# Reordering VectorE's work in a two-layer MLP behind chunked attention, with another loading of the first heads and earlier first matmuls

## The chip, the cores and the metric

The kernel runs on one core of a Trainium2 chip. The metric is the device time of one execution in microseconds (us), as the median over several runs. The engines are called PE (TensorE: matmuls and transposes), ACT (ScalarE), DVE (VectorE), POOL (GpSimd) and SP (SyncE, which here only starts DMAs). Each works through its own list of instructions in order; they wait for each other through semaphores. SBUF is the on-chip memory that all read and write, PSUM the small memory into which PE writes.

## The reference

Attention over chunks, for 4 batches, 8 heads, 768 positions and 64 elements per head; each chunk of 32 queries sees 16 positions to the left, its own 32, 8 to the right and 8 memory rows. Then an MLP over the 3072 tokens with 512 inputs and 2048 hidden units.

```
for c in range(nc):                       # 24 chunks of 32
    l_start, r_end = max(0, 32*c - 16), min(S, 32*c + 32 + 8)
    k_full = concatenate([mem_k, k[:, :, l_start:r_end]], axis=2)
    v_full = concatenate([mem_v, v[:, :, l_start:r_end]], axis=2)
    a = softmax(q_c @ k_full.T / sqrt(64))
    out[:, :, 32*c:32*c + 32] = a @ v_full
x = out.transpose(0, 2, 1, 3).reshape(3072, 512)
h = x @ w_in                              # 512 -> 2048
s = sin(alpha * h)
g = h + s * s / (alpha + 1e-09)
return g @ w_out                          # 2048 -> 512, fp32
```

## The kernel before

The work goes batch by batch, 768 tokens each. Three kinds of stage follow one another.

**Attention burst** (`burst`). Eight blocks of 96 queries (three chunks each). Per block, `qk_exp` makes scores on PE (tile `sc`) and exponentials on ACT (`pt`); `pv` multiplies with v on PE (`ot`) and normalizes on DVE (`rinv`, `x_blk`); `xt` transposes the result on PE and DVE copies it into `xT`, the MLP's input, 96 columns at a time. The three steps of one block lie `lag` iterations apart. In the burst of batch 0, a dummy matmul (`spin`, tile `z`) goes into each iteration.

**First layer** (`l1`, 16 steps, one for each 128 hidden units, called ft). Eight matmuls (4 slices of the 512 inputs, kt, times 2 halves of the tokens) fill a PSUM tile `hT`; ACT computes u = sin(alpha h); the square s2 of u is made by ACT, DVE or POOL, by a letter of a string ("A", "D", "P"; line 460); DVE combines it with `hT` to `gT` (L367). In batch 0 steps 3, 7 and 11 use two small PSUM tiles `hs` instead of `hT` (`split`).

**Second layer** (`l2`). Six blocks of 128 tokens, 16 matmuls each, into a PSUM tile `o`; each block is copied to `o_sb`, in turn by DVE (L400) and ACT (L402), and stored by SP. It is a generator: `Stream.take(n)` issues its next n matmuls, so that the second layer of a batch is spread over the next batch's transposes, burst and first layer.

What sets the order is the program's text: the schedule is written by hand, and the instructions of an engine run as they are emitted. In step ft of the first layer the order is: `stream.take` (2 matmuls of the second layer, 3 in the last batch; a finished block's copy comes with them), in batches 1 and 2 on even ft a `piece` (transposes of one head pair of k or q for the batch after: `t_k` L242 with copies to `kTi` on DVE, L243 and L249; `t_q` L257 with a copy on ACT, L258; the pairs are brought together by `pair_up`, L226, on POOL), and then the whole of `l1` with its square and `gT`.

PSUM tiles come from two pools: `big`, three buffers, holds `hT`, `sc`, `ot` and some transposes; `smp`, two buffers, holds `o`, `hs`, `z` and, in the first-layer stages, the transposes (`tt_a`). A tile that is asked for waits until the last readers of the tile that had the buffer are done: `hT` of a step waits for `gT` of three `hT` tiles before. The SBUF pool `mlp` has three buffers for each of `u`, `s2` and `o_sb`.

Almost all loads are issued by POOL[...]: k and q of batch 0 by head pairs (four of each), v of batch 0 in 16 issues (L125, L129), w_in in 8 pieces of 256 columns (L212), k and q of batch 1, w_out in 4 pieces of 4 ft each (L218), v of batch 1 in four issues (L139 to L148). These queue loads share eight semaphores in turn, and an issue waits until the load eight before it has landed. After the loads, POOL makes copies of head pairs and the "P" squares. The first pairs are brought together (`pr`) by DVE and ACT, transposed, and the burst of batch 0 begins.

Of the kernel before, what the change touches and what calls it, by code (L numbers as in the profile page):

```python
# [9 lines left out]
P = 128  # L10
# [4 lines left out]
F32 = mybir.dt.float32  # L15
ACTF = mybir.ActivationFunctionType
ALU = mybir.AluOpType
# [28 lines left out]
def kernel(  # L46
# [12 lines left out]
    nc = tc.nc  # L59
    B, H, S, D = q.shape  # L60
# [6 lines left out]
    KT = d_model // P  # L67
    NSUB = S // P
    HALF = S // 2
# [121 lines left out]
    for c0, c1, thr, val in (  # L191
# [4 lines left out]
            out=biasm[:, c0:c1], in_=biasm[:, c0:c1],  # L196
# [11 lines left out]
    for pt in pts:  # L208
        nc.vector.memset(pt[:, H * QW:H * QW + 32], 0.0)

    def load_w_in(c):
        nc.gpsimd.dma_start(  # L212
            w_in_sb[:, :, 256 * c:256 * c + 256],
            moe_w_in[:, 256 * c:256 * c + 256].rearrange("(kt p) f -> p kt f", p=P),
        )

    def load_w_out(c):
        nc.gpsimd.dma_start(  # L218
            w_out_sb[:, 4 * c:4 * c + 4, :],
            moe_w_out[512 * c:512 * c + 512].rearrange("(ft p) o -> p ft o", p=P),  # L220
        )


    def pair_up(src, hp, eng=None):
        pr = blk.tile([P, 6, 2, D], BF, name="pr")
        (eng or nc.gpsimd.tensor_copy)(  # L226
            pr[:].rearrange("p r e d -> p e r d"), src[:, 2 * hp:2 * hp + 2]
        )
        return pr

# [80 lines left out]
    def burst(b, stream, shares, lag):  # L311

        xT = xp.tile([P, KT, S], BF, name="xT")
        ptl, xbl = {}, {}
        for s in range(NJ + lag + 1):
            n = shares[s] if s < len(shares) else 0
            if s < NJ:
                ptl[s] = qk_exp(s)
            if b == 0:
                spin(1)  # L320
            stream.take(n // 3, True)
            if 0 <= s - lag < NJ:
                xbl[s - lag] = pv(b, s - lag, ptl.pop(s - lag))
# [9 lines left out]
    def l1(i, ft, xT, gT, sq, split=False):  # L333
        if split:
            hts = [smp.tile([P, 512], F32, name="hs", tag="sm") for _ in range(2)]
        else:
            hT = big.tile([P, 2, 512], F32, name="hT", tag="big")
            hts = [hT[:, 0], hT[:, 1]]
        for kt in range(KT):
            for hf in range(2):  # L340
                nc.tensor.matmul(  # L341
                    hts[hf][:, 0:HALF],
                    w_in_sb[:, kt, P * ft:P * ft + P],
                    xT[:, kt, HALF * hf:HALF * hf + HALF],
                    start=(kt == 0), stop=(kt == KT - 1),
                )
        u = mlp.tile([P, 2, HALF], F32, name="u")
        if split:
            for hf in range(2):
                nc.scalar.activation(  # L350
                    u[:, hf], hts[hf][:, 0:HALF], ACTF.Sin, scale=alpha_sb[:, ft:ft + 1])
        else:
            nc.scalar.activation(u[:], hT[:, :, 0:HALF], ACTF.Sin, scale=alpha_sb[:, ft:ft + 1])  # L353
        s2 = mlp.tile([P, 2, HALF], F32, name="s2")
        if sq == "A":
            nc.scalar.activation(s2[:], u[:], ACTF.Square)  # L356
        else:
            (nc.vector if sq == "D" else nc.gpsimd).tensor_tensor(  # L358
                out=s2[:], in0=u[:], in1=u[:], op=ALU.mult)
        gv = gT[:, ft, :].rearrange("p (e c) -> p e c", e=2)  # L360
        for hf in range(2):
            if split:
                nc.vector.scalar_tensor_tensor(
                    out=gv[:, hf], in0=s2[:, hf], scalar=inv_alpha[:, ft:ft + 1],
                    in1=hts[hf][:, 0:HALF], op0=ALU.mult, op1=ALU.add)
            elif hf == 0:
                nc.vector.scalar_tensor_tensor(  # L367
                    out=gv, in0=s2[:], scalar=inv_alpha[:, ft:ft + 1],
                    in1=hT[:, :, 0:HALF], op0=ALU.mult, op1=ALU.add)

    def l2(i, gT, last=False):
        for s in range(NSUB):
# [32 lines left out]


    first = [nc.vector.tensor_copy, nc.scalar.copy] * 2 + [nc.vector.tensor_copy] * 4
    prs = [pair_up(kq[n], 0, first[n]) for n in range(2)]
    for n in range(2 * HP):
        (t_k if n % 2 == 0 else t_q)(prs[n], n // 2)  # L410
        spin(2)
# [24 lines left out]
    xT = burst(0, stream, (), 2)  # L436
    put_memk(1)
    put_memv(1)

    for i in range(B):  # L440
        gT = gp.tile([P, FT, S], BF, name="gT")
        last = i == B - 1
        at_ft = {2 * n: n for n in range(8)}
        pieces = []
        if not last:
            srcs = [(kq_next[n % 2], n // 2) for n in range(2 * HP)]
        state["pools"] = 1

        def pair_to(n):
            while len(pieces) < min(n, 2 * HP):  # L450
                pieces.append(pair_up(*srcs[len(pieces)], nc.vector.tensor_copy if i == 0 and len(pieces) % 2 == 0 else None))

        def piece(n):
            pair_to(n + 3)
            (t_k if n % 2 == 0 else t_q)(pieces[n], n // 2)

        if 0 < i < B - 1:
            pair_to(2)
        for ft in range(FT):
            sq = ("ADADADAAADADADAA" if i == 0 else "ADAAPDADADAPADAD")[ft]  # L460
            if 1 <= ft:
                stream.take(3 if last else 2)
            if 0 < i < B - 1 and ft in at_ft:
                piece(at_ft[ft])
            if i == 0 and ft == 14:
                pair_to(3)
            l1(i, ft, xT, gT, sq, i == 0 and ft in (3, 7, 11))
        stream.add(l2(i, gT, last))
        if not last:
            if i == 0:  # L470
                state["pools"], state["t"] = 3, 0
                stream.take(4)
# [12 lines left out]
            if i + 2 < B:  # L485
                load_v_all(i + 2)
                put_memv(i + 2)
# [31 lines left out]
```

The softmax here doesn't subtract the row's maximum and nothing guards it: scores larger than these inputs give would overflow.

## Time and profile before

| | |
|---|---|
| median of 8 runs | 243.73 us (243.23 to 245.54) |
| the profiled execution, own time | 243.65 us |
| its span (first to last instruction) | 241.9 us |
| granted clock of PE | full in all slices |
| head: loads, transposes of batch 0 | 0 to 16 us |
| burst of batch 0 | 16 to 28 |
| first layer of batch 0 | 28 to 52 |
| transposes for batch 1, with second layer of batch 0 | 52 to 62 |
| burst of batch 1 / first layer | 62 to 81 / 81 to 113 |
| burst of batch 2 / first layer | 113 to 135 / 135 to 167 |
| burst of batch 3 / first layer | 167 to 189 / 189 to 217 |
| second layer of batch 3, end | 217 to 242 |

The stages are read from the timeline, from the first matmul of one kind to the first of the next. A matmul is called by its line (L341 first layer, L393 second layer, L266 scores, L288 attention times v). The page gives a mean of 326 ns for a first-layer matmul, but that is its duration from start to end in a pipeline; eight in a row take 1.30 us in the chain of waits, 0.163 us each. Of the waits, those of PE count: an idle time of another engine costs nothing unless PE waits for it later.

### The profile page before, as it was taken

To read this page: it belongs to the slowest core of one execution; us is meant where nothing else is said; L and a number is where in the kernel's file an instruction comes from. 1 tells how busy PE (TensorE), PEld (TensorE's weight loads), DVE (VectorE), ACT (ScalarE), POOL (GpSimd) and SP (SyncE) were. 2 spreads that over 40 slices of the span, in tenths; PEclk is the share of its full clock that TensorE was granted. 3 is DMA by queue.
4 is the path that set the end of the run, shared out by engine and by line. 5 is a ranking of instruction groups with operands and counts; after the bars stand their busy time and mean duration, and the time that the engine had idled before them with its cause. 6 is when DMAs were issued, how large, how long until landed. Compare 5 with 4: busy or idle time off the path is not lost.

```text
span 241.9 us, 4498 instructions
## 1 busy us (share of the span) xinstructions
PE 220.4 (91%) x1785; PEld 122.1 (50%) x1785; DVE 160.1 (66%) x287; ACT 154.5 (64%) x237; POOL 72.7 (30%) x96
## 2 busy tenths in 40 slices
PE   7698899988989979898999996998999999899994
PEld 2345465545445555454455653554455555454453
DVE  3577979998268667969557686968557267876100
ACT  3499499973884467788563774778764775871000
POOL 8899865213912114148300114120000002020000
PEclk9999999999999999999999999999999999999999
DMA  7999999999999910009994101001111101101122
GB/s 79 163 119 88 155 186 204 207 204 125 167 220 135 120 46 0 36 9 154 172 144 89 46 0 43 0 3 43 46 43 47 43 0 46 43 0 43 43 89 87
DMA packets 53852, 21.11 MB, mean 87 GB/s; under 512 B 36296, under 2 KB 50888, under 8 KB 53832
## 3 DMA queue, kind: packets, MB, share of 16 engines
q0 software_dynamic: 47616, 14.40, 73.2%
q1 hardware_dynamic: 6216, 6.43, 9.1%
q8 instruction: 14, 0.23, 0.4%
q14 instruction: 6, 0.05, 0.1%
HBM read 28.91 MB, written 6.29 MB: 146 GB/s over the span
## 4 chain that ended last, share of the span: by engine, by line
PE 44%; DMA 15%; DVE 13%; issue 11%; POOL 9%; ACT 7%; POOLq 1%; DVEq 0%; ACTq 0%
PE o L393 26%; DMA w_out_sb<-in_moe_w_out_dram 9%; PE hT L341 8%; DVE gT L367 6%; DVE s L358 4%; DMA w_in_sb<-in_moe_w_in_dram 4%; POOL vw L125 3%; ACT u L353 3%; PE ot L288 3%; PE sc L266 3%; POOL s L358 2%; DMA q_bf<-in_q_dram 2%; POOL vw L129 2%; ACT s L356 2%; ACT pt L275 2%
## 5 line engine op out<-in xcount | busy, mean ns | idle before, releaser
L393 PE MATMUL o<-w_out_sb,gT 128*128 128x512 bf16 x368 | 98.7, 380 | 1.5 <-DMA w_out_sb<-in_moe_w_out_dram 0.9
L341 PE MATMUL hT<-xT,w_in_sb 128*128 128x384 bf16 x488 | 87.5, 326 | 3.9 <-DVE gT L367 3.6
L367 DVE SCALAR_TENSOR_TENSOR gT<-s,inv_alpha,hT 128x768 bf16<-128x768 f32 x61 | 61.1, 1012 | 28.9 <-ACT s L356 20.4
L353 ACT ACTIVATE u<-hT,alpha_sb 128x768 f32<-128x768 f32 x61 | 54.6, 897 | 26.7 <-PE hT L341 25.5
L341 PEld LDWEIGHTS <-w_in_sb 128*128 128x128 bf16 x512 | 49.4, 98 | 38.7 <-issue 5.9
L275 ACT ACTIVATE pt<-sc,biasm 128x256 bf16<-128x256 f32 x96 | 37.5, 492 | 13.1 <-PE sc L266 13.1
L393 PEld LDWEIGHTS <-gT 128*128 128x128 bf16 x368 | 31.8, 98 | 26.4 <-DVE gT L367 1.4
L358 POOL TENSOR_TENSOR s<-u 128x768 f32<-128x768 f32 x6 | 8.8, 1466 | 73.7 <-ACT u L353 73.7
L356 ACT ACTIVATE s<-u 128x768 f32<-128x768 f32 x34 | 28.7, 843 | 1.1
L358 DVE TENSOR_TENSOR s<-u 128x768 f32<-128x768 f32 x24 | 24.6, 1025 | 0.4 <-ACT u L353 0.3
L293 DVE TENSOR_TENSOR x_blk<-ot,rinv 96x512 bf16<-96x512 f32 x32 | 22.0, 687 | 1.1
L226 POOL COPY pr<-q_bf 128x768 bf16<-128x768 bf16 x12 | 10.0, 837 | 41.9 <-PE tt_a L242 24.8
L292 DVE RECIPROCAL rinv<-ot 96x8 f32<-96x8 f32 x32 | 6.5, 202 | 20.0 <-PE ot L288 19.6
L402 ACT COPY o_sb<-o 128x512 f32<-128x512 f32 x11 | 6.4, 585 | 20.0 <-PE o L393 20.0
L400 DVE COPY o_sb<-o 128x512 f32<-128x512 f32 x12 | 8.3, 688 | 16.1 <-PE o L393 16.1
L288 PEld LDWEIGHTS <-pt 128*128 128x128 bf16 x256 | 11.9, 98 | 7.2 <-issue 2.3
L171 PE MATMUL z<-zeros 128*128 128x512 bf16 x37 | 13.5, 452 | 1.3 <-DVE zeros L165 1.3
L288 PE MATMUL ot<-vw,pt 128*128 128x65 bf16 x256 | 13.0, 193 | 0.8 <-ACT pt L275 0.6
L266 PEld LDWEIGHTS <-kTi 64*128 64x128 bf16 x256 | 6.9, 94 | 13.0 <-issue 6.6
L257 PEld LDWEIGHTS <-pr 128*128 128x128 bf16 x96 | 6.2, 97 | 14.1 <-issue 7.8
L266 PE MATMUL sc<-qT,kTi 64*128 64x96 bf16 x256 | 11.4, 205 | 1.8 <-ACT pt L275 1.2
L306 PEld LDWEIGHTS <-x_blk 96*128 96x128 bf16 x128 | 8.4, 97 | 6.6 <-DVE x_blk L293 1.5
(66 smaller groups left out, 181.2 us busy)
## 6 DMA issues: line engine op xcount, KB each, us to landing
out_dram<-o_sb SPq DMA_DIRECT2D x23, 256.0 KB, 2.3
k_bf<-in_k_dram POOLq DMA_DIRECT2D x3, 768.0 KB, 9.2
q_bf<-in_q_dram POOLq DMA_DIRECT2D x3, 768.0 KB, 14.0
vw<-in_v_dram POOLq DMA_DIRECT2D x6, 384.0 KB, 18.3
w_in_sb<-in_moe_w_in_dram POOLq DMA_DIRECT2D x8, 256.0 KB, 7.7
w_out_sb<-in_moe_w_out_dram POOLq DMA_DIRECT2D x4, 512.0 KB, 19.0
k_bf<-in_k_dram POOLq DMA_DIRECT2D x4, 192.0 KB, 6.0
q_bf<-in_q_dram POOLq DMA_DIRECT2D x4, 192.0 KB, 6.5
```

The costliest lines, as they stand in the source:

```text
L171: nc.tensor.matmul(z[:], zeros[:, 0:P], zeros[:])
L226: (eng or nc.gpsimd.tensor_copy)(pr[:].rearrange("p r e d -> p e r d"), src[:, 2 * hp:2 * hp + 2])
L266: nc.tensor.matmul(sc[:, e, QW * hp:QW * hp + QW], kTi[64 * e:64 * e + 64, hp, 104 * j:104 * j + P], qT[64 * e:64 * e + 64, hp, QW * j:QW ...
L275: nc.scalar.activation(pt[:, 0:H * QW].rearrange("p (g e c) -> p e g c", g=4, e=2)[:, :, :, 32 * m:32 * m + 32], sc[:, :, 0:4 * QW].rearra ...
L288: nc.tensor.matmul(otv[:, h // 4, h % 4, :], pt[:, QW * h:QW * h + P], vws[b % 2][:, h, j, 0:D + 1])
L293: nc.vector.tensor_tensor(out=x_blk[:].rearrange("p (g e) d -> p g e d", g=2), in0=otv[0:QW, :, :, 0:D], in1=rv.unsqueeze(3).to_broadcast( ...
L341: nc.tensor.matmul(hts[hf][:, 0:HALF], w_in_sb[:, kt, P * ft:P * ft + P], xT[:, kt, HALF * hf:HALF * hf + HALF], start=(kt == 0), stop=(kt ...
L353: nc.scalar.activation(u[:], hT[:, :, 0:HALF], ACTF.Sin, scale=alpha_sb[:, ft:ft + 1])
L356: nc.scalar.activation(s2[:], u[:], ACTF.Square)
L358: (nc.vector if sq == "D" else nc.gpsimd).tensor_tensor(out=s2[:], in0=u[:], in1=u[:], op=ALU.mult)
L367: nc.vector.scalar_tensor_tensor(out=gv, in0=s2[:], scalar=inv_alpha[:, ft:ft + 1], in1=hT[:, :, 0:HALF], op0=ALU.mult, op1=ALU.add)
L393: nc.tensor.matmul(o[:], gT[:, ft, P * s:P * s + P], w_out_sb[:, ft, :], start=(ft == 0), stop=(ft == FT - 1),)
```

## The change

Five things are done together.

1. `l1` no longer emits the square on DVE and `gT`. It returns them as a function `finish`, which is called in the next step after `stream.take` and `piece`, ahead of that step's matmuls (after the loop for the last step). Squares on ACT and POOL stay where they were.
2. The squares of batch 0 go from ten on ACT and six on DVE to eight on ACT, four on DVE and four on POOL. The last batch takes 2 second-layer matmuls per step instead of 3.
3. The first head pair of k and q is loaded without a cast, fp32, by SP's and ACT's queues into two buffers of the pool tag `u`; the copies to `pr` read fp32. POOL has six loads of k and q pairs left.
4. w_in is loaded in five pieces (256, 256, then three of 512 columns), w_out in two of 8 ft each.
5. In the burst of batch 0, a hook issues the first-half matmuls (4 of 8) of ft 0 and ft 1 in iteration 9 (before and after the transposes of block 6) and of ft 2 in iteration 10 (after those of block 7). `l1` later issues the other half alone.

```diff
@@ -178,7 +178,11 @@
     kq = alloc_qk()
-    load_qk_pair(0, 0, *kq)
+    kq0 = []
+    for src, eng in ((k, nc.sync), (q, nc.scalar)):
+        f = mlp.tile([P, 2, HALF], F32, name="u")
+        eng.dma_start(f[:], src[0, 0:2].rearrange("h (p r) d -> p h (r d)", p=P))
+        kq0.append(f)
     masks.make_identity(nc, ident[:])
@@ -208,23 +212,25 @@
-    def load_w_in(c):
+    def load_w_in(c0, c1):
...
-            w_out_sb[:, 4 * c:4 * c + 4, :],
-            moe_w_out[512 * c:512 * c + 512].rearrange("(ft p) o -> p ft o", p=P),
+            w_out_sb[:, 8 * c:8 * c + 8, :],
+            moe_w_out[1024 * c:1024 * c + 1024].rearrange("(ft p) o -> p ft o", p=P),
...
@@ -323,27 +329,36 @@
+            if hook:
+                hook(s, 0, xT)
             stream.take((n + 1) // 3, True)
             if 0 <= s - lag - 1 < NJ:
                 xt(xT, s - lag - 1, *xbl.pop(s - lag - 1))
+            if hook:
+                hook(s, 1, xT)
             stream.take((n + 2) // 3, True)
...
+    def l1_mm(hts, ft, xT, kt, hf):
+        nc.tensor.matmul(
+            hts[hf][:, 0:HALF],
+            w_in_sb[:, kt, P * ft:P * ft + P],
+            xT[:, kt, HALF * hf:HALF * hf + HALF],
+            start=(kt == 0), stop=(kt == KT - 1),
+        )
+
+    def l1(ft, xT, gT, sq, hts, halves, split=False):
         for kt in range(KT):
...
+            for hf in halves:
+                l1_mm(hts, ft, xT, kt, hf)
...
+        elif sq == "P":
+            nc.gpsimd.tensor_tensor(out=s2[:], in0=u[:], in1=u[:], op=ALU.mult)
+
+        def finish():
+            if sq == "D":
+                nc.vector.tensor_tensor(out=s2[:], in0=u[:], in1=u[:], op=ALU.mult)
+            gv = gT[:, ft, :].rearrange("p (e c) -> p e c", e=2)
...
+                elif hf == 0:
+                    nc.vector.scalar_tensor_tensor(
+                        out=gv, in0=s2[:], scalar=inv_alpha[:, ft:ft + 1],
+                        in1=hT[:, :, 0:HALF], op0=ALU.mult, op1=ALU.add)
+
+        return finish
...
-    for c in range(8):
-        load_w_in(c)
+    for c0, c1 in ((0, 256), (256, 512), (512, 1024), (1024, 1536), (1536, 2048)):
+        load_w_in(c0, c1)
     kq_next = load_qk(1)
-    for c in range(4):
+    for c in range(2):
         load_w_out(c)
...
+    def early(s, point, xT):
+
+        ft = {(9, 0): 0, (9, 1): 1, (10, 1): 2}.get((s, point))
+        if ft is not None:
+            opened[ft] = l1_open(ft)
+            for kt in range(KT):
+                l1_mm(opened[ft], ft, xT, kt, 0)
+
+    xT = burst(0, stream, (), 2, early)
...
+        finish = None
         for ft in range(FT):
-            sq = ("ADADADAAADADADAA" if i == 0 else "ADAAPDADADAPADAD")[ft]
+            sq = ("ADADAAPADPADPAPA" if i == 0 else "ADAAPDADADAPADAD")[ft]
             if 1 <= ft:
-                stream.take(3 if last else 2)
+                stream.take(2)
             if 0 < i < B - 1 and ft in at_ft:
                 piece(at_ft[ft])
             if i == 0 and ft == 14:
                 pair_to(3)
-            l1(i, ft, xT, gT, sq, i == 0 and ft in (3, 7, 11))
+            if finish is not None:
+                finish()
+            split = i == 0 and ft in (3, 7, 11)
+            if ft in opened:
+                finish = l1(ft, xT, gT, sq, opened.pop(ft), (1,))
+            else:
+                finish = l1(ft, xT, gT, sq, l1_open(ft, split), (0, 1), split)
+        finish()
         stream.add(l2(i, gT, last))
```

`l1_open` asks for the PSUM tiles of a step, as `l1` did before.

More of the change, by code (lines that the diff above doesn't have):

```diff
@@ L209 @@
         nc.vector.memset(pt[:, H * QW:H * QW + 32], 0.0)
-    def load_w_in(c):
+    def load_w_in(c0, c1):
         nc.gpsimd.dma_start(
-            w_in_sb[:, :, 256 * c:256 * c + 256],
-            moe_w_in[:, 256 * c:256 * c + 256].rearrange("(kt p) f -> p kt f", p=P),
+            w_in_sb[:, :, c0:c1],
+            moe_w_in[:, c0:c1].rearrange("(kt p) f -> p kt f", p=P),
         )
@@ L226, in pair_up @@
         (eng or nc.gpsimd.tensor_copy)(
-            pr[:].rearrange("p r e d -> p e r d"), src[:, 2 * hp:2 * hp + 2]
+            pr[:].rearrange("p r e d -> p e r d"),
+            src[:].rearrange("p h (r d) -> p h r d", d=D) if hp is None
+            else src[:, 2 * hp:2 * hp + 2],
         )
@@ L309, in xt, with burst @@
         nc.vector.tensor_copy(xT[:, :, QW * j:QW * j + QW], xtp)
-    def burst(b, stream, shares, lag):
+    def burst(b, stream, shares, lag, hook=None):
         xT = xp.tile([P, KT, S], BF, name="xT")
@@ L328, in burst, with l1_open @@
                 xt(xT, s - lag - 1, *xbl.pop(s - lag - 1))
+            if hook:
+                hook(s, 1, xT)
             stream.take((n + 2) // 3, True)
         return xT
-    def l1(i, ft, xT, gT, sq, split=False):
+    def l1_open(ft, split=False):
         if split:
[L335 to L338, printed above, removed]
-        for kt in range(KT):
[L340 to L346, printed above, removed]
+            return [smp.tile([P, 512], F32, name="hs", tag="sm") for _ in range(2)]
+        hT = big.tile([P, 2, 512], F32, name="hT", tag="big")
+        return [hT[:, 0], hT[:, 1], hT]
+    def l1_mm(hts, ft, xT, kt, hf):
[6 more added lines that the diff above has]
+    def l1(ft, xT, gT, sq, hts, halves, split=False):
+        for kt in range(KT):
+            for hf in halves:
+                l1_mm(hts, ft, xT, kt, hf)
+        hT = None if split else hts[2]
         u = mlp.tile([P, 2, HALF], F32, name="u")
@@ L356, in l1 @@
             nc.scalar.activation(s2[:], u[:], ACTF.Square)
[L357 to L369, printed above, removed]
+        elif sq == "P":
[4 more added lines that the diff above has]
+            gv = gT[:, ft, :].rearrange("p (e c) -> p e c", e=2)
+            for hf in range(2):
+                if split:
+                    nc.vector.scalar_tensor_tensor(
+                        out=gv[:, hf], in0=s2[:, hf], scalar=inv_alpha[:, ft:ft + 1],
+                        in1=hts[hf][:, 0:HALF], op0=ALU.mult, op1=ALU.add)
+                elif hf == 0:
+                    nc.vector.scalar_tensor_tensor(
+                        out=gv, in0=s2[:], scalar=inv_alpha[:, ft:ft + 1],
+                        in1=hT[:, :, 0:HALF], op0=ALU.mult, op1=ALU.add)
+        return finish
     def l2(i, gT, last=False):
@@ L407 @@
     first = [nc.vector.tensor_copy, nc.scalar.copy] * 2 + [nc.vector.tensor_copy] * 4
-    prs = [pair_up(kq[n], 0, first[n]) for n in range(2)]
+    prs = [pair_up(kq0[n], None, first[n]) for n in range(2)]
     for n in range(2 * HP):
@@ L435 @@
     stream = Stream()
-    xT = burst(0, stream, (), 2)
+    opened = {}
+    def early(s, point, xT):
[5 more added lines that the diff above has]
+    xT = burst(0, stream, (), 2, early)
     put_memk(1)
```

## The prediction

> **What bounds the kernel now.** I read the page's busy shares first, then the chain of waits, then the stages in windows, and in each stage the waits of TensorE (PE). The own time of the profiled execution is 243.65 us, its span 241.9 us, so 1.75 us lie around it; the median of the eight runs is 243.73 us, the same within 0.1 us. I sum against 243.65.
>
> From the page, and then from the windows:
>
> ```profile
> span 241.9 us, 4498 instructions
> PE 220.4 (91%) x1785; PEld 122.1 (50%) x1785; DVE 160.1 (66%) x287; ACT 154.5 (64%) x237; POOL 72.7 (30%) x96
> ```
>
> ```profile
> 81.00:113.00 32.00, 28.13 (x198) 16.71 (x195) 24.39 (x34) 23.96 (x29) 12.29 (x13) 1.00 0.25 44
> 113.00:135.00 22.00, 22.00 (x236) 11.54 (x231) 14.30 (x31) 13.43 (x29) 3.22 (x5) 1.00 1.69 138
> 135.00:167.00 32.00, 28.71 (x194) 16.80 (x192) 24.02 (x33) 22.39 (x27) 7.11 (x7) 1.00 0.06 20
> 167.00:190.00 23.00, 22.96 (x239) 11.74 (x238) 13.74 (x30) 15.13 (x31) 0.00 (x0) 1.00 0.12 45
> 190.00:222.00 32.00, 30.47 (x171) 16.47 (x170) 22.75 (x24) 21.07 (x25) 2.93 (x2) 1.00 0.05 19
> ```
>
> The columns after the window are its length and the busy time of PE, weight loads, VectorE (DVE), ScalarE (ACT) and GpSimd (POOL). PE fills the attention bursts (113 to 135, 167 to 190) and has holes in the first-layer stages. A PE hole in any later stage is paid in full, and one that is closed is won in full, because a full burst follows. The waits of PE in the first-layer stages of batches 1 and 2 say who makes the holes:
>
> ```profile
> PE tt_a L257 <- DVE o_sb L400: 1.4, 1, 1.4
> PE hT L341 <- DVE gT L367: 1.0, 2, 0.5
> PE tt_a L257 <- DVE kTi L249: 1.0, 1, 1.0
> PE sc L266 <- DVE gT L367: 0.5, 1, 0.5
> ...
> PE tt_a L257 <- DVE o_sb L400: 1.7, 1, 1.7
> PE tt_a L257 <- DVE kTi L249: 1.4, 2, 0.9
> ```
>
> The timeline of VectorE around the 1.7 us shows the cause:
>
> ```profile
> 143.53 1.01 DVE L367 SCALAR_TENSOR_TENSOR gT<-s,inv_alpha,hT 128x768 bf16<-128x768 f32 x1 [0.72 <-ACT s L356]
> 144.47 0.85 DVE L243 COPY kTi<-tt_a 128x672 bf16<-128x672 bf16 x1
> 145.24 0.31 DVE L249 COPY kTi<-tt_a 128x48 bf16<-128x48 bf16 x2
> 146.27 1.01 DVE L367 SCALAR_TENSOR_TENSOR gT<-s,inv_alpha,hT 128x768 bf16<-128x768 f32 x1 [0.73 <-POOL s L358]
> 147.20 0.68 DVE L400 COPY o_sb<-o 128x512 f32<-128x512 f32 x1
> ```
>
> The copy of o stands behind a gT that itself waits for a square on GpSimd. o was complete near 144.0; its copy starts at 147.20, and the transposes that need its PSUM buffer start at 147.94.
>
> Batch 0 is different. From 30.4 to 54.7 ScalarE and VectorE are both full (27 to 57: 22.89 and 27.17 of 30 us), and beside them runs the load of the weights; the chain of waits has
>
> ```profile
> 26.05 8.68 DMA w_in_sb<-in_moe_w_in_dram
> 34.73 0.28 issue
> 35.01 21.65 DMA w_out_sb<-in_moe_w_out_dram
> ```
>
> [...]
>
> **Part 1, VectorE's part of a step behind the next step's evacuations.** Nothing is added; the square (0.95 us) and gT (1.01) of step ft go behind the o copy (0.69) and the kTi copies (0.85 + 0.31) that step ft+1 emits.
>
> Batch 1. First matmul of ft 0 at 81.09, first score of the next burst at 112.78: 31.7 us. Work: 128 first-layer matmuls at 1.30 us per 8 are 20.8, 18 of L2 at 1.08 per 5 are 3.9, 7 transposes at 0.34 are 2.4; sum 27.1, so 4.6 us are holes. Placed by hand: 1.52 before the transposes at 85.91 (o copy), 1.16 before those at 101.82 (kTi, copied at 100.60 though transposed at 97.6), and 1.5 to 1.7 near the end (hT at 108.87 and 110.79, score at 112.78). The first two vanish: the o copy can run at 82.9 and the kTi copy at 97.9. What is late next is gT, whose hT buffer is wanted three steps later. From the end of hT(ft) PE has two steps of 1.30, up to three takes of 0.43 and one or two transposes of 0.34 before it wants the buffer, 3.3 to 4.4 us; Sin 0.90, square 0.84 to 1.47 and gT 1.01 need 2.8 to 3.5, with a kTi pair in front 1.16 more. So I expect 0.4 us of new stall near ft 10 and still 0.8 at ft 14, behind the GpSimd square of ft 11; the score's wait stays 0.4. Gain 4.6 - 1.6 = 3.0 us.
>
> Batch 2. 134.69 to 167.49 is 32.8; work 20.8 + 26 x 0.215 = 5.6 + 2.4 = 28.8; 4.0 of holes (2.2 around 145 to 148, 0.73 at 156.26, 1.04 at 164.46). All have an evacuation queued behind a gT; new stall 0.4 at ft 10, and I keep 0.4 more for VectorE's squares, which took up to 1.49 instead of 0.95 us beside GpSimd copies. Gain 3.2 us.
>
> **Part 2, two L2 matmuls per step in the last batch instead of three.** Now the 26 left-over matmuls are gone by ft 9, and from 206.6 on PE runs 1.30 us steps against VectorE's (16 x 1.01 + 6 x 0.95 + 1.4)/16 = 1.45: holes of 1.09 at 211.58, 0.4 at 214.60, 0.5 at 221.03, 2.0 in all. At two they last to ft 13 and a step is 1.73 us on PE, above VectorE. What stays is the end: gT(15) is ready about 3.5 us after the last hT, the L2 matmuls before it take 15 x 0.215 = 3.2; 0.3 remains. Gain 1.6 us (0.8 to 1.9).
>
> **Part 3, the start and batch 0.** The first pair of k and q by SP's and ACT's queues takes two issues (0.94 and 0.73) off GpSimd. Before, k lands at 5.66 and q at 7.73; on a hardware queue the nearest row is the out store of 256 KB at 2.3 us from issue to landing, so near 4 us. ACT then does the table load and memk copy first, so q's copy starts near 6.0 instead of 7.73. But loads run back to back to 14.2 (VectorE waits 0.55 for the last q at 14.66), so the end moves by less: I take 1.2 us (0.4 to 1.7) for the first score at 16.1. GpSimd reaches w_in 1.5 us earlier.
>
> The 12 early matmuls (0.16 each) fill PE gaps of 0.2 to 0.5 us near 27 and 28, but Sin of ft 0 needs both halves and starts no sooner, and then ScalarE and VectorE are the limit. Worth nothing; if w_in were late there, they would push the last xT back, up to 1 us; the first chunk, issued at 20.9, lands 4.2 us later (shortest w_in row) and is wanted near 25.9.
>
> The squares go from 10 on ACT, 6 on DVE to 8, 4 and 4 on POOL. DVE has 22.5 - 2 x 0.95 = 20.6 us left. By queue order the first GpSimd square (ft 6) ends near 40.8 where DVE is free at 39.4: 1.4 us of the 1.9 are lost, and gT(15) moves only with the start, from 54.74 to some 54. This needs GpSimd to be free at 39. Now it stands at 41.55 and 45.41 in a v issue that waits for k and q. With 5 and 2 issues for w_in and w_out instead of 8 and 4, the v issues wait for w_in chunks instead, in the compiled order, and GpSimd is free near 36.
>
> The weights: w_in starts 1.5 us earlier and moves in longer runs; DMA now gives 145 GB/s from 24 to 28 and 204 on w_out. I take 0.5 us for that and the last w_out at 54.6 instead of 56.66. But with halves instead of quarters the 9th L2 matmul waits for it, where it was the 13th: one more transpose-and-three-matmul piece, 0.98 us, stands behind. Net 1.0 us at the first score of batch 1 (61.92 to 60.9; 0.0 to 2.3).
>
> **Sum.** 1.0 + 3.0 + 3.2 + 1.6 = 8.8 us; 243.65 - 8.8 = 234.85, I say 234.9.
>
> **Rivals.**
> - *The wait moves from o and kTi to gT.* For: the slack of 3.3 to 4.4 us against 2.8 to 4.7 is thin, and VectorE is 24 of 32 us busy, a higher share if the stage shrinks. Against: only four k pieces a batch. Half of part 1 is lost: 3.1 us, 238.0. Chance 0.20.
> - *All holes close and the start goes through.* Then 4.6 + 4.0 + 2.0 and 1.8 of batch 0: 231.3. Against: the GpSimd squares keep their latency. Chance 0.12.
> - *GpSimd isn't free at 39* and stays in its issues to 46.2 as now: the square ends at 47.7 instead of 40.8, all of batch 0 waits 6.9 us: 241.8. Against: the new order of waits. Chance 0.07.
> - *Slower.* The kTi copy now stands at the head of VectorE's queue and waits for PE, whose transposes come behind a whole step. Place: every evacuation in the first-layer stages of batches 1 to 3. If each pushes gT past the slack, PE pays 4 x 1.16 + 2 x 0.69 = 6.0 us in batches 1 and 2 each and 2 x 0.69 = 1.4 in batch 3, 13.4 in all on top of the forecast: 234.85 + 13.4 = 248.2. It decides from where a k transposition is done later than the Sin of the step before; in the trace it is done about 0.8 us after that step's matmuls, the Sin only after 0.9, which speaks against it. Chance 0.05.
>
> **How the numbers follow.** Forecast 0.56, own range 233.0 to 237.0; the rest as above. The range takes in the first rival and most of the second: 232.0 to 239.3. About 0.5%, 1.2 us, is what a measurement of this kernel tells from no change: faster 0.93, within 0.02 (the third rival's edge and little effects that cancel), slower 0.05.
>
> **What would show it.** Part 1: in the stages of batches 1 and 2 PE's waits for the o copy and kTi are gone, the stages last near 28.7 and 29.6 us. Part 2: no hole over 0.4 us between the last batch's ft 9 and 15. Part 3: the first score near 15, the three v issues no longer waiting for k and q, the last w_out near 54.6, the first score of batch 1 near 60.9. Wrong would be new waits of hT for gT above 1 us a batch, or a GpSimd square that starts after 41.

## The result and the profile after

| | before | after |
|---|---|---|
| median | 244.54 us (32 runs, 243.08 to 245.91) | 239.51 us (11 runs, 238.63 to 240.22) |
| profiled execution, own time | 243.65 us | 239.2 us |
| its span | 241.9 us | 237.2 us |

The ratio of the means is 0.9803, 95% interval 0.9778 to 0.9827. The change is faster, by about 2% (the interval leaves open on which side of 2%): 4.7 us of span, where the sum said 8.8. Of 48 fast executions of the kernel before that were timed beside the experiments, 26 show a mean granted clock of PE of 0.993 or less and have a median of 245.37 us, the other 22, like the profiled one, 0.999 or more and 243.66 us; all 12 executions of the changed kernel show 0.991 or less. The page after begins so, and the last of these lines is PE's granted clock in 40 slices:

```profile
span 237.2 us, 4495 instructions
PE 220.3 (93%) x1785; PEld 123.2 (52%) x1785; DVE 159.5 (67%) x285; ACT 151.9 (64%) x235; POOL 73.2 (31%) x93
...
PEclk9889999999999999999999999999999999999998
```

PE has the same busy time as before (220.3 against 220.4 us), so the gain is holes that closed. New is the 8 in the second and third slice, roughly 6 to 18 us: in the head PE ran at less than full clock. (The 8 at the end lies behind the last matmul.)

To see where the gain came and went, I read from both timelines the first score and the first first-layer matmul of each batch, and took differences:

| stretch | before | after | gain | forecast |
|---|---|---|---|---|
| start to first score, batch 0 | 16.11 | 18.57 | -2.46 | +1.2 |
| to first score, batch 1 | 45.81 | 46.21 | -0.40 | -0.2 |
| to its first layer | 19.01 | 19.01 | 0 | 0 |
| first layer of batch 1 | 31.85 | 28.52 | +3.33 | +3.0 |
| burst of batch 2 | 21.91 | 21.93 | -0.02 | 0 |
| first layer of batch 2 | 32.80 | 29.51 | +3.29 | +3.2 |
| burst of batch 3 | 21.79 | 21.57 | +0.22 | 0 |
| first layer of batch 3, to the end | 52.62 | 51.88 | +0.74 | +1.6 |

The gains add up to 4.7 us. The two middle stages did what was forecast. The head did the opposite.

The windows of the first-layer stages of batches 1, 2 and 3 after (columns as before):

```profile
81.00:113.00 32.00, 31.14 (x223) 18.70 (x222) 26.82 (x38) 24.21 (x30) 11.71 (x12) 1.00 0.29 51
...
135.00:167.00 32.00, 31.41 (x215) 18.50 (x213) 26.65 (x35) 26.08 (x33) 6.55 (x7) 1.00 0.05 17
...
190.00:222.00 32.00, 31.45 (x171) 16.47 (x170) 21.35 (x23) 19.14 (x23) 2.93 (x2) 1.00 0.09 33
```

PE is busy 31.1 and 31.4 of 32 us in the first two, where it was 28.1 and 28.7. PE's waits, in the windows 0 to 30, 30 to 62, 81 to 113, 110 to 167 and 190 to 238, in this order (total, times, longest):

```profile
PE tt_b L263 <- ACT pr L230: 3.3, 1, 3.3
...
PE hT L350 <- DVE gT L385: 3.6, 5, 1.5
...
PE hT L350 <- DVE gT L385: 0.7, 2, 0.6
...
PE sc L272 <- DVE gT L385: 0.6, 1, 0.6
...
PE o L413 <- DVE gT L385: 0.4, 1, 0.4
```

The waits for `o_sb` and `kTi` in the stages of batches 1 and 2 are gone; what is left there is 0.7 and 0.6 us for gT. The first line is the failure: PE waits 3.3 us for ACT's copy of the first q pair. Before, the window 0 to 30 had

```profile
PE tt_b L257 <- ACT pr L226: 2.0, 2, 1.2
```

VectorE at the place where the 1.7 us hole was:

```profile
142.28 0.85 DVE L249 COPY kTi<-tt_a 128x672 bf16<-128x672 bf16 x1
143.05 0.31 DVE L255 COPY kTi<-tt_a 128x48 bf16<-128x48 bf16 x2
143.28 1.00 DVE L385 SCALAR_TENSOR_TENSOR gT<-s,inv_alpha,hT 128x768 bf16<-128x768 f32 x1
144.20 0.68 DVE L420 COPY o_sb<-o 128x512 f32<-128x512 f32 x1
145.82 1.01 DVE L385 SCALAR_TENSOR_TENSOR gT<-s,inv_alpha,hT 128x768 bf16<-128x768 f32 x1 [0.94 <-POOL s L373]
```

The gT that waits for a GpSimd square stands there still and waits 0.94 us. But the o copy now runs in front of it, so its wait is no longer PE's.

The head, by the timelines of ACT before (three lines) and after (three lines), and then PE after:

```profile
3.70 1.28 ACT L200 ACT_TABLE_LOAD   x1 [3.70 <-DMA memk_f<-in_mem_k_dram]
4.99 0.62 ACT L200 CAST memk_bf<-memk_f 32x512 bf16<-32x512 f32 x1
7.73 0.83 ACT L226 COPY pr<-q_bf 128x768 bf16<-128x768 bf16 x1 [2.13 <-DMA q_bf<-in_q_dram]
```

```profile
7.89 1.28 ACT L204 ACT_TABLE_LOAD   x1 [7.89 <-DMA memk_f<-in_mem_k_dram]
9.18 0.62 ACT L204 CAST memk_bf<-memk_f 32x512 bf16<-32x512 f32 x1
9.71 0.82 ACT L230 CAST pr<-u 128x768 bf16<-128x768 f32 x1
...
10.59 0.82 PE L263 MATMUL tt_b<-ident,pr 128*128 128x128 bf16 x6 [3.30 <-ACT pr L230]
```

The mem_k rows landed at 7.89 instead of 3.70 us, although SP issues their four loads only 0.5 us later than before (from 1.31 instead of 0.81). ACT's queue has the table load and the mem_k copy ahead of the copy of q. So q's copy started at 9.71 instead of 7.73, with q itself long there, as the second experiment will show. Then came a second loss. PE's clock in windows of 1 us (the third column from the end):

```profile
9.00:10.00 1.00, 0.00 (x0) 0.00 (x0) 0.00 (x0) 0.99 (x3) 1.00 (x2) 1.00 1.58 190
10.00:11.00 1.00, 0.41 (x5) 0.42 (x6) 0.00 (x0) 0.53 (x1) 1.00 (x3) 0.71 1.57 189
11.00:12.00 1.00, 1.00 (x6) 0.36 (x4) 0.00 (x0) 0.55 (x1) 1.00 (x2) 0.50 1.63 172
12.00:13.00 1.00, 1.00 (x11) 0.77 (x11) 0.45 (x2) 0.98 (x2) 0.93 (x2) 0.50 2.18 120
13.00:14.00 1.00, 1.00 (x8) 0.47 (x6) 0.73 (x2) 0.00 (x0) 0.84 (x2) 0.59 2.34 141
```

At the end of the wait PE's clock falls to half; by the shares 0.71 and 0.59 of the two mixed windows this lasts from 10.4 to 13.8. Six transposes then take 0.82 us where the same take 0.50 at full clock. The drop is 3.4 us long and stands behind a wait of 3.30 us. But runs 2 and 4 will show the same drop behind shorter waits (1.17 and 0.69 us, and 1.47 us); the last section comes back to it.

### The profile page after: what moved, and what is told of

Same layout as the page of the kernel before. It is cut to its first block, busy times and chain, and to the rows that moved or that the text cites. A ratio compares the mean times of both kernels' runs of the same rounds, so it can differ in the third digit from the quotient of the medians.

```text
span 237.2 us, 4495 instructions
## 1 busy us (share of the span) xinstructions
PE 220.3 (93%) x1785; PEld 123.2 (52%) x1785; DVE 159.5 (67%) x285; ACT 151.9 (64%) x235; POOL 73.2 (31%) x93
## 4 chain that ended last, share of the span: by engine, by line
PE 62%; ACT 11%; DVE 10%; issue 7%; POOL 7%; DMA 1%; POOLq 1%; DVEq 0%; ACTq 0%
PE o L413 30%; PE hT L350 20%; DVE gT L385 5%; ACT pt L281 4%; ACT u L368 4%; PE ot L294 3%; PE sc L272 3%; DVE s L377 2%; POOL s L373 2%; PE ot L312 2%; PE o L402 1%; ACT s L371 1%; DMA vw<-in_v_dram 1%; POOL vw L125 1%; POOL k_bf L102 1%
## 5 line engine op out<-in xcount | busy, mean ns | idle before, releaser
L368 ACT ACTIVATE u<-hT,alpha_sb 128x768 f32<-128x768 f32 x61 | 54.6, 898 | 27.3 <-PE hT L350 27.3
L373 POOL TENSOR_TENSOR s<-u 128x768 f32<-128x768 f32 x10 | 14.7, 1469 | 83.6 <-ACT u L368 73.3
L371 ACT ACTIVATE s<-u 128x768 f32<-128x768 f32 x32 | 27.0, 843 | 1.0
L377 DVE TENSOR_TENSOR s<-u 128x768 f32<-128x768 f32 x22 | 24.1, 1097 | 0.5 <-ACT u L368 0.5
L171 PE MATMUL z<-zeros 128*128 128x512 bf16 x37 | 14.6, 485 | 1.3 <-DVE zeros L165 1.3
L263 PEld LDWEIGHTS <-pr 128*128 128x128 bf16 x96 | 6.9, 101 | 7.6 <-ACT pr L230 4.0
## 6 DMA issues: line engine op xcount, KB each, us to landing
w_in_sb<-in_moe_w_in_dram POOLq DMA_DIRECT2D x3, 512.0 KB, 10.4
```

The lines of the kernel that those rows point to most:

```text
L171: nc.tensor.matmul(z[:], zeros[:, 0:P], zeros[:])
L373: nc.gpsimd.tensor_tensor(out=s2[:], in0=u[:], in1=u[:], op=ALU.mult)
L377: nc.vector.tensor_tensor(out=s2[:], in0=u[:], in1=u[:], op=ALU.mult)
```

## The experiments

All runs were timed in five rounds, each against the kernel before on the same chip. They form four sets (1 to 4, 5 to 8, 9 and 10, 11), in which the kernel before had medians of 245.55, 244.01, 243.75 and 244.70 us: small differences of medians from set to set say little, and stages are compared in the profiled executions. "First score" is that of batch 0; "stretch" is from there to the first score of batch 1.

**1. mem_k's loads ahead of k's on SP.** Is it the order on SP's queue that made mem_k late?

```diff
+    for b in range(B):
+        nc.sync.dma_start(memk_f[NM * b:NM * b + NM], mem_k[b].rearrange("h n d -> n h d"))
     for src, eng in ((k, nc.sync), (q, nc.scalar)):
         f = mlp.tile([P, 2, HALF], F32, name="u")
...
-    for b in range(B):
-        nc.sync.dma_start(memk_f[NM * b:NM * b + NM], mem_k[b].rearrange("h n d -> n h d"))
```

> The changed kernel with one edit: SP issues the four loads of mem_k ahead of the fp32 load of k. Theory A (the head lost 2.5 us because mem_k lands late behind k on SP's queue, and ScalarE's table load and mem_k copy stand ahead of the copy of q): mem_k lands near 3.7 us, the copy of q starts near 5.6 to 6 instead of 9.7, the first score comes near 16 instead of 18.6, and the whole takes 2 to 2.6 us less than the changed kernel, near 237. Theory B (the fp32 loads crowd the DMA engines, so all loads of the head land later whatever the order): the first score stays past 17.5 and the time within 1 us of 239.5.

239.48 us, ratio 0.9759 (0.9711 to 0.9808); first score at 19.80. ACT and VectorE in its timeline:

```profile
5.53 1.28 ACT L204 ACT_TABLE_LOAD   x1 [5.53 <-DMA memk_f<-in_mem_k_dram]
6.83 0.62 ACT L204 CAST memk_bf<-memk_f 32x512 bf16<-32x512 f32 x1
7.35 0.82 ACT L230 CAST pr<-u 128x768 bf16<-128x768 f32 x1
...
9.41 0.56 DVE L230 CAST pr<-u 128x768 bf16<-128x768 f32 x1 [6.32 <-DMA u<-in_k_dram]
```

mem_k came at 5.53, not at 3.70, and now k came at 9.41, 7.1 us after its issue at 2.28. So the order decides who is late, but not that someone is: with the two fp32 loads in the first microseconds, the small loads and the large ones get into each other's way, and theory B had the numbers. From 2 to 8 us the loads move 113 GB/s before and 227 after. PE waits 4.4 us for k's copy here, and its clock is at half from 8.8 to 15.6 us, which is part of the 19.80.

**2. q's copy ahead of mem_k's on ACT.** If ACT's order is what makes q's copy late, this mends it without touching a load.

```diff
-    nc.scalar.copy(memk_bf[:], memk_f[:])
...
     prs = [pair_up(kq0[n], None, first[n]) for n in range(2)]
+    nc.scalar.copy(memk_bf[:], memk_f[:])
```

> The changed kernel with one edit: on ScalarE the copy of the first q pair stands ahead of the copy of mem_k; the loads are issued as in the changed kernel. Theory A: the table load runs before 3 us, q is copied near 5.2 to 6.1 us, the mem_k copy still waits to 7.9 and holds the first qT copy to 8.5; first score near 16 to 16.5, time near 237. Theory B: the first score stays past 17.5, the time near 239.5.

235.75 us, ratio 0.9606 (0.9562 to 0.965), 3.8 us below the changed kernel. ACT's timeline:

```profile
1.31 1.28 ACT L229 ACT_TABLE_LOAD   x1 [1.31 <-PEq L541]
...
5.42 0.83 ACT L229 CAST pr<-u 128x768 bf16<-128x768 f32 x1 [2.83 <-DMA u<-in_q_dram]
...
7.98 0.62 ACT L428 CAST memk_bf<-memk_f 32x512 bf16<-32x512 f32 x1 [1.73 <-DMA memk_f<-in_mem_k_dram]
```

q landed at 5.42, 4.6 us after its issue at 0.81 and 1.4 us later than I had taken. mem_k is as late as in the changed kernel (7.98), and now it delays only its own transposes. The table load went along with the first ACT copy to 1.31, where nothing waits. In this profiled execution the PE clock was at 0.5 from 11.0 to 14.4 us, and the first score came only at 16.11. The clock fell after waits of PE of 1.17 and 0.69 us, both shorter than the changed kernel's 3.30. In the later runs with this head (5, 6, 8, 10 and 11) it stayed at 1.0 there, and the score came at 14.28, 14.45, 14.46, 14.27 and 14.96.

**3. The first pair by GpSimd, as before.**

```diff
-    kq0 = []
-    for src, eng in ((k, nc.sync), (q, nc.scalar)):
...
+    load_qk_pair(0, 0, *kq)
...
-    prs = [pair_up(kq0[n], None, first[n]) for n in range(2)]
+    prs = [pair_up(kq[n], 0, first[n]) for n in range(2)]
```

> The changed kernel with the first head pair of k and q loaded as before (cast to bf16, by GpSimd), all else as changed. Both theories: the first score back near 16.1, 2.5 us less than the changed kernel, near 237.0. If it stays near 239.5, the head's loss is made up in batch 0 by the weights or by VectorE, and the head is not what failed.

236.70 us, ratio 0.9652 (0.9611 to 0.9692); first score at 15.59, so the new loading, in the form in which it was made, cost 3 us of the head. But batch 1 began at 63.09, since the weights are asked for later than in the changed kernel (w_out at 27.4 and 28.2 instead of 25.5 and 26.4); PE's waits between 30 and 62 have

```profile
PE o L409 <- DMA w_out_sb<-in_moe_w_out_dram: 1.8, 1, 1.8
```

until 56.67. The last w_out landed there before the change too (56.66), although it was asked for only at 35.0: larger pieces and earlier issues alone don't bring it earlier here, they only make the 9th second-layer matmul wait for it instead of the 13th.

**4. The deferral alone**, on the kernel before: `l1` returns `finish`, with the square on VectorE and `gT` in it.

```diff
+            if finish is not None:
+                finish()
-            l1(i, ft, xT, gT, sq, i == 0 and ft in (3, 7, 11))
+            finish = l1(i, ft, xT, gT, sq, i == 0 and ft in (3, 7, 11))
+        finish()
```

> The kernel before with VectorE's part of a first-layer step put behind the next step's evacuations and nothing else. If the 3.3 us that the first-layer stages of batches 1 and 2 won each come from this part alone: stages of 28.5 and 29.5 us, first score at 16.1, and 243.65 - 6.6 = near 237, faster than the whole change. If they need the other parts: over 239.

236.94 us, ratio 0.9663 (0.9621 to 0.9705). The first layers of batches 1 and 2 last 28.52 and 29.51 us, to the hundredth as in the changed kernel. One of five edits gives 6.9 us of span (241.9 to 235.0), more than all five together. In this execution the PE clock was at half from 8.9 to 12.3 us, although the head is that of the kernel before and PE's longest wait for a q copy in it was 1.5 us.

**5. Run 2 with batch 0's squares as before.**

```diff
-            sq = ("ADADAAPADPADPAPA" if i == 0 else "ADAAPDADADAPADAD")[ft]
+            sq = ("ADADADAAADADADAA" if i == 0 else "ADAAPDADADAPADAD")[ft]
```

> The kernel with q copied first on ScalarE (e2), with batch 0's squares put back as before (ten on ScalarE, six on VectorE, none on GpSimd). From its first score to the first score of batch 1 e2 takes 46.2 us, the kernel with the deferral alone 45.3. Theory S (the GpSimd squares cost: VectorE waits 1.9 us for three of them, and one VectorE square beside a GpSimd square takes 2.2 us instead of 0.95): back near 45.3 or less, 234.8 in all. Theory N (the squares gained what their fewer instructions promise, and the loss lies in the early matmuls or the load pieces): 46.2 or more, 235.8 or more.

234.69 us, ratio 0.9607 (0.957 to 0.9643). By the time, 1.06 us below run 2, this is theory S; by the stretch, 46.34 us against 46.23, it is theory N. But the two profiled executions differ in the head: run 2's, with its half clock, began batch 0 1.83 us later. PE's waits show part of what happened: hT waits for gT 2.3 us instead of 3.6, but o waits 1.4 for w_out, where run 2 has no such wait. One wait took the other's place, and how much of that is the earlier start is not shown.

**6. Run 2 without the early matmuls.**

```diff
-    xT = burst(0, stream, (), 2, early)
+    xT = burst(0, stream, (), 2)
```

> The kernel with q copied first on ScalarE (e2), without the first-layer matmuls issued within the burst of batch 0. If they are worth nothing, as forecast, because Sin of ft 0 needs both halves: within 0.3 us of e2, 235.75. If they fill PE's gaps with use: 0.8 to 1.2 us slower; if they hold the last xT back: 0.5 us faster.

235.42 us, ratio 0.963 (0.9595 to 0.9665); the stretch is 46.36 against 46.23. The twelve early matmuls are worth nothing that can be measured.

**7. The deferral and two second-layer matmuls per step in the last batch**, on the kernel before.

```diff
-                stream.take(3 if last else 2)
+                stream.take(2)
```

> The kernel before with the deferral (e4) and two instead of three second-layer matmuls per step in the last batch. In the whole change the stage from the last batch's first hT to its main second-layer matmuls took 30.7 us, in e4 31.75. If that is the two takes' doing: 30.7 here and 1.1 us less than e4, near 235.85. If the change's other parts did it: as e4, 236.94.

235.91 us, ratio 0.9656 (0.9619 to 0.9694). From the last first layer's start to the end of the span it takes 51.56 us, in run 4 52.65: 1.1 us for this edit. These two edits together give 8.0 us of span (241.9 to 233.9, both at full clock). The forecast for them was 3.0 + 3.2 + 1.6 = 7.8.

**8. Run 2 with w_in in eight pieces and w_out in four**, as before. It tests the third rival, that GpSimd isn't free for its squares.

```diff
-            w_out_sb[:, 8 * c:8 * c + 8, :],
-            moe_w_out[1024 * c:1024 * c + 1024].rearrange("(ft p) o -> p ft o", p=P),
+            w_out_sb[:, 4 * c:4 * c + 4, :],
+            moe_w_out[512 * c:512 * c + 512].rearrange("(ft p) o -> p ft o", p=P),
...
-    for c0, c1 in ((0, 256), (256, 512), (512, 1024), (1024, 1536), (1536, 2048)):
+    for c0, c1 in [(256 * c, 256 * c + 256) for c in range(8)]:
         load_w_in(c0, c1)
...
-    for c in range(2):
+    for c in range(4):
         load_w_out(c)
```

> The kernel with q copied first on ScalarE (e2), with w_in in eight pieces and w_out in four again, the GpSimd squares kept. Forecast's third rival: GpSimd stands in its v issues until k and q of batch 1 have landed near 44 to 46, its first square starts then instead of at 39.9, batch 0 loses 4 to 6 us: 240 to 242. If GpSimd gets free near 36 to 38 anyway: within 1 us of 235.75.

241.93 us, ratio 0.9912 (0.9884 to 0.994), 6.2 us above run 2. GpSimd's timeline:

```profile
39.96 0.78 POOL L145 DMA_DIRECT2D vw<-in_v_dram  x1 [2.50 <-DMA k_bf<-in_k_dram]
43.86 0.83 POOL L148 DMA_DIRECT2D vw<-in_v_dram  x1 [3.12 <-DMA q_bf<-in_q_dram]
44.72 1.48 POOL L372 TENSOR_TENSOR s<-u 128x768 f32<-128x768 f32 x1
```

The last two v issues wait for k and q of the next batch, the first square behind them starts at 44.72, and VectorE's gT and PE wait for it (7.7 and 6.7 us, the longest of each). In the changed kernel the same issues wait for w_in and are through at 36.4. Behind PE's wait its clock is at half from 44.7 to 51.5 us, so the 6.2 us have that price in them.

**9. A busy gap.** How much of the head is the clock? The changed kernel with more dummy matmuls behind the first k transposes.

```diff
         (t_k if n % 2 == 0 else t_q)(prs[n], n // 2)
-        spin(2)
+        spin(14 if n == 0 else 2)
```

> The changed kernel with 14 dummy matmuls instead of 2 behind the first k transposes, so that PE works through most of the 3.3 us in which it waited for q's copy. Theory A (the wait costs twice: the lateness itself, and then the PE clock of 0.5 from 10.7 to 13.6, which stretches six transposes from 0.50 to 0.82 us and a pair of dummies from 0.59 to 1.06): the clock stays at 1.0 in the head, q's copy still starts near 9.7, the first score comes at 17.3 to 17.8 instead of 18.57, and the time is 0.8 to 1.2 us below that of the changed kernel, near 238.4. Theory B (the head from q's copy on is paced by ACT's and DVE's copies and the low clock costs nothing): first score within 0.3 us of 18.57 although the clock is full, time near 239.5.

237.94 us, ratio 0.9762 (0.9722 to 0.9802), 1.6 us below the changed kernel; first score at 17.19 instead of 18.57. PE's window after the gap:

```profile
10.00:11.00 1.00, 0.43 (x7) 0.43 (x8) 0.00 (x0) 0.52 (x1) 1.00 (x3) 1.00 1.55 190
11.00:12.00 1.00, 1.00 (x14) 0.54 (x12) 0.23 (x1) 0.88 (x2) 1.00 (x2) 1.00 1.64 175
```

The clock is 1.00 where it was 0.71 and 0.50; in 11 to 12 PE does 14 matmuls instead of 6. q's copy starts at 9.69, as late as without the dummies. So the half clock cost 1.4 us of the head, a little more than theory A said (a first score at 17.3 to 17.8), and theory B falls. Five of the six executions took 237.82 to 238.13 us at a mean granted clock of 0.998 or more, the sixth 239.81 at 0.993: the dummies made the drop rare, but did not rule it out.

**10. The best of the parts**: q's copy first, old squares, no early matmuls, w_in in five pieces and w_out in four (the edits of runs 2, 5 and 6, and the w_out lines of run 8). Against run 5:

```diff
-            w_out_sb[:, 8 * c:8 * c + 8, :],
+            w_out_sb[:, 4 * c:4 * c + 4, :],
...
-    for c in range(2):
+    for c in range(4):
         load_w_out(c)
...
-    xT = burst(0, stream, (), 2, early)
+    xT = burst(0, stream, (), 2)
```

> The run with q's copy first and batch 0's old squares (234.69 us), now without the early matmuls and with w_out in four quarters instead of two halves; w_in stays in five pieces. Theory A (in that run the 1.4 us that the second layer waited for w_out were made by the halves: the 9th matmul wants the second half, with quarters the 13th wants the last quarter, one transpose-and-three-matmul piece or 0.98 us later): no wait or one under 0.5 us for w_out, the stretch from the first score of batch 0 to that of batch 1 falls from 46.34 to 45.3 to 45.8, the time is near 233.9. Theory B (gT(15), from ACT's and DVE's work on ten and six squares, ends the stretch as much as the weights do): the wait moves from w_out to gT, the stretch stays within 0.3 of 46.34, the time within 0.4 of 234.7.

234.25 us, ratio 0.9604 (0.9567 to 0.9641); the stretch is 45.31 us, no wait for w_out is left, gT is waited for 1.4 us. This is theory A by the stage (45.3 to 45.8). The medians, 0.44 us apart, are too near to each other to say it alone. It is below both kernels of the case.

**11. Run 10 with the new squares.** Do GpSimd's squares themselves hold batch 0 back?

```diff
-            sq = ("ADADADAAADADADAA" if i == 0 else "ADAAPDADADAPADAD")[ft]
+            sq = ("ADADAAPADPADPAPA" if i == 0 else "ADAAPDADADAPADAD")[ft]
```

> The run with q's copy first, no early matmuls and w_out in quarters (234.25 us, stretch from the first score of batch 0 to that of batch 1 45.31 us), with one edit: batch 0's squares as in the changed kernel, 8 on ACT, 4 on DVE and 4 on POOL, instead of 10 and 6. Theory A (the GpSimd squares themselves hold batch 0 back, by their latency of 1.5 us and by slowing a DVE square beside them from 0.95 to 2.2): hT waits for gT 3 us or more instead of 1.4, the stretch is 46.1 to 46.5, the time near 235.2. Theory B (batch 0 is ended by the weights, whichever engine squares): the stretch stays within 0.3 of 45.31, the time within 0.4 of 234.25.

241.75 us, ratio 0.9891 (0.9847 to 0.9934); the stretch is 51.18. Neither theory: it is run 8 again, by w_out's four pieces alone, with PE's clock at half from 46.4 to 49.8 us behind a wait of 5.2 us.

```profile
42.91 0.83 POOL L148 DMA_DIRECT2D vw<-in_v_dram  x1 [3.06 <-DMA q_bf<-in_q_dram]
43.77 1.48 POOL L372 TENSOR_TENSOR s<-u 128x768 f32<-128x768 f32 x1
```

I had left out of my expectation that two more issues move v's two places on in the eight semaphores, from w_in's pieces to k and q (L145 waits 2.58 us for k, L148 3.06 for q). So the question that it was made for, what the squares cost with w_out in quarters and GpSimd free, stays open. What it does show, with runs 5, 6 and 10, is how two edits hang together:

| stretch in us | w_out in halves | w_out in quarters |
|---|---|---|
| old squares | 46.34 (with early matmuls) | 45.31 |
| new squares | 46.36 | 51.18 |

In quarters GpSimd is blocked to 43.7, which the old squares don't feel and the new ones do.

## Why the prediction was right and wrong

**Part 1, right.** 3.33 and 3.29 us for 3.0 and 3.2, and run 4 ascribes both to the deferral alone. The waits for the o and kTi copies went. What the forecast kept as new stall for gT (1.6 us with the score's wait in batch 1) was 0.7 for hT by PE's waits. The first rival, that the wait moves to gT, did not come about, nor did the slower one: no k transposition pushed a gT past its slack.

**Part 2, right in kind, too large.** 1.07 us for 1.6. From the last batch's first hT to the second-layer matmul that waits for the last gT it took 31.75 us before and in run 4, 30.68 in run 7 and in the changed kernel. The term that was mis-sized is what remains. By the starts of the matmuls, the holes before were 2.0 us, as the forecast had them, but one of 0.28 before 209.58 and one of 0.59 before 216.00 are left, where I had counted 0.3 in all: the last gT is there 3.8 us after the last hT (212.18 to 216.00), not 3.5. In the changed kernel the tail behind the last copy on VectorE was 0.3 us longer, which leaves 0.74; no run shows why.

**Part 3, wrong, and this is the error.** The two first parts alone end at 233.9 us of span (run 7), the whole change at 237.2: part 3 costs 3.3 where it should have given 1.0 (3.0 at the first score of batch 1, 64.78 against 61.80 in run 7, and the 0.3 of the tail). The step that failed is this: "ACT then does the table load and memk copy first, so q's copy starts near 6.0 instead of 7.73." It took mem_k's landing at 3.70 from the trace before and left it there, while the change put two fp32 loads of 384 KB into the same microseconds, one of them ahead of it on its own queue. mem_k landed at 7.89, and the copy started at 9.71. By run 1, where mem_k stands ahead of k and lands at 5.53, 2.4 us of the delay are its place behind k and 1.8 the other loads beside it. q itself landed at 5.42 (run 2), not near 4. Run 1 shows that being first on a queue isn't enough: mem_k landed there at 5.53 instead of 3.70 although nothing stood ahead of it on its own queue. My forecast had no such delay in it, neither for the loads that were moved nor for the ones beside them. (The fp32 copy itself is a small part: 0.57 us on VectorE, where the bf16 copy of a pair takes 0.35.)

The head splits like this. With q's copy first and a full clock the first score is at 14.3 to 15.0 (runs 5, 6, 8, 10 and 11), 1.2 to 1.8 us earlier than the 16.11 before; the forecast had 1.2, to 1.7 at most. (The old head isn't a fixed point either: 15.59 in run 3, 15.73 in run 7.) mem_k ahead of q puts it at 17.19 (run 9), 2.2 to 2.9 us later. The half clock adds 1.38 (18.57). I had costed a wait of PE in the head as its length and no more; there it had a second price, and neither the trace before, at full clock with waits for q's copies of 1.2 us at the longest, nor my list of unknown costs had that in it. The price is not the change's alone: run 4, with the old head, shows the drop too, and so by their mean clock do over half of the executions of the kernel before, though only profiled ones show where it fell. The change made it certain (12 of 12 executions); with q's copy first it came in 1 of 24 (runs 2, 5, 6 and 10).

**Batch 0.** The stretch got 0.40 us longer, forecast 0.2. GpSimd is free at 36.4 as forecast (near 36), its first square starts at 42.35, after the 41 that the prediction named as a sign of being wrong, but only because all of batch 0 is later (39.89 in run 2, whose first score came 2.46 us earlier). w_out isn't waited for at all: of its two issues at 25.5 and 26.4 the slower took 27.3 us, so it was there by 53.7 (forecast 54.6). But hT waits for gT 3.6 us, the other sign that was named. Before, PE's waits between 30 and 62 were

```profile
PE hT L341 <- DVE gT L367: 1.4, 2, 1.1
PE o L393 <- DMA w_out_sb<-in_moe_w_out_dram: 0.9, 1, 0.9
```

GpSimd, VectorE and PE in the timeline after:

```profile
43.84 1.01 DVE L385 SCALAR_TENSOR_TENSOR gT<-s,inv_alpha,hT 128x768 bf16<-128x768 f32 x1 [1.25 <-POOL s L373]
...
45.77 1.47 POOL L373 TENSOR_TENSOR s<-u 128x768 f32<-128x768 f32 x1 [1.96 <-ACT u L368]
...
45.82 2.22 DVE L377 TENSOR_TENSOR s<-u 128x768 f32<-128x768 f32 x1
...
49.22 4.06 PE L350 MATMUL hT<-xT,w_in_sb 128*128 128x384 bf16 x24 [1.54 <-DVE gT L385]
```

A square on VectorE that starts 0.05 us after one on GpSimd takes 2.22 us, not 0.95: it ends 0.80 after GpSimd's. So a "P" in the string takes 0.95 us off VectorE and can put 1.3 back on its neighbour. The forecast, which gave 0.4 for such things in batch 2, had none in batch 0. What such squares cost the whole stretch is not shown; runs 5 and 11 leave it open.

**The rivals.** The time, 239.51, lies 0.2 us above the range and between the first and the third rival, but by neither's mechanism. The second, in which all holes close and the start goes through, failed with the head. The third was real but excluded by this change's own pieces: run 8 prices it at 6.2 us, with a half clock in it, where the prediction said 6.9. The case that was missing is a head that gets later through a load that nobody edited.

## What to carry to other kernels

When a load is moved to another queue, write down every load issued within a few microseconds of it and ask what waits for each: the one that gets late can be a 16 KB load that the diff doesn't touch, and what it costs is all that stands behind its reader on an in-order engine (here q's copy, which started 2.0 us later than before). Order the first copies on an engine by when their data land after the change, not before it, and price the half clock that can follow waits of PE: it came behind 3.30 us of waits in the changed kernel, where it lasted 3.4 us and cost 1.4, and behind 1.86 us in all in run 2. Take a bundle of edits apart before believing in it: here one of five edits gave more than the five together, and two that look independent (piece sizes and squares) hang together: the new squares lost some 5 us with w_out in quarters.

## What was not expected of the hardware

- Loads of several queues in the first microseconds: mem_k's rows landed 4.2 us later (3.70 to 7.89) for an issue that came 0.5 us later, and in run 1 the fp32 k took 7.1 us from issue to landing, where in the changed kernel it was there at 5.15, 4.3 us after its issue at 0.81.
- PE's half clock. Six profiled executions have a drop before the last matmul: the changed kernel and runs 1, 2, 4, 8 and 11. The drops last 3.4 us, in runs 1 and 8 twice that. In the 3.4 us just before the drop PE was busy for 0.29, 0.23, 1.63, 1.50, 0.00 and 0.01 us; in run 2 (7.6 to 11.0) this holds two waits, 1.17 and 0.69 us. In run 11 a stretch of the same length, 39.5 to 42.9, has 1.58 us of work and no drop at its end; the drop there comes at 46.4. So 1.58 went without a drop and 1.63 had one: the two are too near to each other, for matmul ends that are modelled, to read a border from these traces. In the head the drops begin at 8.8, 8.9, 10.4 and 11.0 us (runs 1 and 4, the changed kernel, run 2). And one program can be hit in one execution and spared in the next: run 2's profiled execution has a mean clock of 0.993, the other five 0.997 or more.
- The first six k transposes took 0.82 us before (at 6.08) and in the changed kernel (at 5.78), as long as at half clock, and 0.51 in runs 2, 3, 4, 7 and 9. PEclk is 1.00 from 0 to 7 us in the changed kernel and in runs 2, 3, 4 and 7 alike: what makes the difference is not shown.
- VectorE's square beside GpSimd's: 2.22 us (45.82 to 48.04, GpSimd's from 45.77 to 47.24), where the median of the changed kernel's 22 is 0.95. It ends 0.80 us after GpSimd's, which is not quite a whole 0.95. What holds it up is not shown.
